# The last segment's attention in the turned form of the other three, a whole-product output projection, and 64-column products in the spectral stage

## The chip, the cores and the metric

The kernel runs on one core of a Trainium2 chip. The metric is the device time of one execution in microseconds (us), the median of several; a profile of a single execution is beside it. The engines are PE (matrix products), PEld (its weight loads), DVE, ACT and POOL (elementwise work), and SP, which here only issues transfers.

## The reference

The input x is 2048 tokens of 640 features in bf16. Two branches are computed from it and mixed by a gate per token.

```python
def _A_ref(x, wq, wk, wv, wo, beta):          # H=32 heads of 20, N=4 segments of L=512
    q, k, v = heads(x @ wq), heads(x @ wk), heads(x @ wv)
    phi = lambda t: jnp.where(t > 0, t + 1.0, jnp.exp(t))
    g = _sigmoid(beta).reshape(1, H, 1, 1)
    for s in range(N):
        logits = jnp.einsum('bhqd,bhkd->bhqk', qs, ks) * scale + mask      # causal in the segment
        a_dot = softmax(logits) @ vs
        a_mem = (phi(qs) @ M) / (phi(qs) @ z + 1e-06)
        outs.append(g * a_mem + (1.0 - g) * a_dot)
        M, z = M + phi(ks).T @ vs, z + phi(ks).sum()
    return o @ wo

def _B_ref(x, w_r, w_i):
    return irfft2(rfft2(x) * (w_r + 1j * w_i))

g = _sigmoid((x * gate_w).sum(-1, keepdims=True))
return g * _A_ref(...) + (1 - g) * _B_ref(...)
```

## The kernel before

**Stages.** The kernel works through four segments s = 0 to 3 of 512 tokens. For each, `project` multiplies x with wq, wk and wv; q and k go through a scratch in memory (`qk_scr`) and come back as rows of one head each (`qkp`), and the values stand in `va`. `mem_read` computes the memory's part (`mem`), `attend` the softmax attention. Branch B (`fft`) is a series of matrix products with tables (`Ac`, `Bt`, `tt`, `Wt`, `Cp`, `big`), whose result stands in `G`; one of them, here called the D product, multiplies `Ac` with `big`. Its pieces are laid between the segments' work all along.

**Attention.** Eight groups of four heads make up a segment, two groups a pair. A pair has five units (`qk_unit`): the products q·k of a unit fill the four PSUM banks of the pool "qk", and ACT takes the exponential of all four (L1508, into `ex`), so each unit waits until the one before it has been read. POOL or DVE set the masked corners to zero (L1540 and L1549, L1539 and L1545). Then the values:

- For segments 0 to 2 `pv_flipped` (L1407): 20 products a group in which the values stand and the probabilities stream, on 32-column tiles of the array, one a head. Their result has a head's 20 values and its sum in rows. It is evicted to `ub`, written to memory (`u_scr`) by pairs, and read back as the features in order (`oU`) and as the sums of all heads (`dnc`, in `denominators`, L1431). The sums are inverted (L1440), joined with the gates (`rc`, L1442) and spread over the features by four products (`spread`, L1446) whose eviction is `r`; `oU` is multiplied by `r` (L1791). The memory's part goes through `o_scr`, is read back transposed (`mT`) and added (L1799).
- For segment 3 `pv_group` (L1556): 40 products a group in which the probabilities stand and 21 columns of values and ones stream. Result and sums lie beside each other, so the division follows at once (`rs`, `on`, L1587 to L1592), `mem` is added (L1597), and `last_transposes` (L1756) turns `on` by 20 products into `oTl`.

**The end.** `finish_tile` (L1773) makes the output of 128 tokens in two halves. One bank collects eight products on 32-column tiles of `G` with the gate's columns (`fbg`, `fbn`) and then the output projection, five chunks of `oU` or `oTl` with `wo`, each chunk in four pieces on 32-column tiles (L546 where a function splits it, L548 for segment 3). The sum is evicted as `ot` and written out.

**Order.** The program is recorded as operations with their dependences; the class `Sched` puts them on the engines in the order of a table of numbers (`ORDER`, L741; `ENDED`, L615, says which end frees a bank), and turns dependences into semaphores. Each engine runs its own row strictly in that order, and so does the queue of transfers that it issues: nearly all are SP's. PE has modes by the shape of its tiles: whole (0), 32-column tiles (2), the q·k shapes (1) and 64-column tiles (4).

Of the kernel before, what the change touches and what calls it, by code (L numbers as in the profile page):

```python
# [9 lines left out]
BF = dt.bfloat16  # L10
# [34 lines left out]
class Op:  # L45
    __slots__ = ("id", "alts", "preds", "succs", "prio", "banks", "nbytes", "npred", "eng", "t0", "t1",
                 "stamp", "rank", "need_inc", "dyn", "first", "outside", "name", "dma", "key", "xfer", "lock", "mode", "emode", "hold", "width", "high", "follow")


class Sched:  # L50
# [9 lines left out]
    def op(self, alts, r=(), w=(), prio=0.0, nbytes=0, name="", after=(), dma=False, xfer=0.0, lock=False, mode=0, hold=False, width=16):  # L60
# [4 lines left out]
        o.high, o.follow = False, None  # L65
# [47 lines left out]
    def schedule(self, pools, order, ended, nsem=56):  # L113
# [17 lines left out]
        for p, o in zip(queue["pool"], queue["pool"][1:]):  # L131
            if p.high != o.high:
                o.follow = p
        pe, held = queue["pe"], {}
        for i, o in enumerate(pe):
            o.emode = o.mode
            if o.mode < 0:
                modes = [held[id(b)] for b in o.banks if id(b) in held]
                if not modes and i and pe[i - 1].emode not in (1, 4):
                    modes = [pe[i - 1].emode]  # L140
                for q in pe[i + 1:] if not modes else ():
                    m = q.mode if q.mode >= 0 else held.get(id(q.banks[0]), -1)
                    if m >= 0:
                        modes = [0 if m == 1 else m]
                        break
                o.emode = (modes + [0])[0]
            if o.emode not in (1, 4):
                for b in o.banks:
                    held[id(b)] = o.emode
# [6 lines left out]
        sems = [[0.0, i, None] for i in range(nsem)]  # L156
        issued = []
        self.order = []
# [49 lines left out]
        while len(self.order) < len(order):  # L208
# [19 lines left out]
            if e == "pe" and o.emode != mode:  # L228
                occ += self.COST[mode, o.emode]
                mode = o.emode  # L230
# [3 lines left out]
            if o.dma:  # L234
                if o.hold:
                    free[e] = max(free[e], max(ring) + 170.0)
                for q in range(o.width):
                    ring[q] = max(ring[q], free[e] + 1300.0) + o.xfer
# [6 lines left out]
                sems.sort(key=lambda q: (q[0], q[1]))  # L245
                sm = sems[0]
# [13 lines left out]
        self.nsem = nsem  # L260
# [235 lines left out]
class Kern:  # L496
# [35 lines left out]
    def mms(self, items, r, w, prio, name="", extra=0.0, mode=0):  # L532
# [861 lines left out]
    def attend(self, s):  # L1394
# [9 lines left out]
        if s < 3:  # L1404
            self.denominators(s)
# [469 lines left out]
```

## Time and profile before

| | |
|---|---|
| median of three runs | 243.16 us (242.58 to 244.0) |
| the profiled execution's own time | 242.17 us |
| its span | 240.4 us, so 1.8 us lie around it |
| PE, DVE, ACT, POOL busy | 95%, 85%, 84%, 39% of the span |
| granted clock of PE | 1.00 throughout |
| transfers | 43.46 MB in 58072 packets |

Rows of groups read: line, engine, operation, output<-inputs, how many | busy us, mean ns of one | idle time of the engine before them, and what ended it. PE's means overlap, since products are pipelined: what one costs is read from the start of a row to the start of the next. Rows of the timeline read: start, busy us, engine and group, and in brackets the idle time before. Rows of transfers end with the median us from issue to landing.

### The profile page before, as it was taken

What the parts mean: (1) busy time and instruction counts of PE and PEld (TensorE: products, weight loads), DVE (VectorE), ACT (ScalarE), POOL (GpSimd) and SP (SyncE); (2) the same over time, 40 slices, a digit from 0 to 9 for tenths busy, and PEclk for the clock granted to TensorE, in tenths of its full rate; (3) what the DMA queues carried; (4) which work ended last, traced back from release to release, by engine and by line L of the source; (5) the groups of instructions that cost most, each with busy time, mean ns of one, the idle gap of its engine ahead of it and who ended that gap; (6) DMA issues with size and microseconds to landing.
All of it is one profiled execution on the core that took longest, in us unless ns stands there. A gap on an engine that the chain in (4) does not pass through costs nothing.

```text
span 240.4 us, 10161 instructions
## 1 busy us (share of the span) xinstructions
PE 228.9 (95%) x4361; PEld 146.3 (61%) x4361; DVE 203.8 (85%) x493; ACT 202.7 (84%) x253; POOL 92.9 (39%) x172
## 2 busy tenths in 40 slices
PE   7999799999999999999989999999999999999993
PEld 4666367666556674654656555565555667667883
DVE  0978888999999899999999999899999679747742
ACT  2398979999999999999999999899899977678630
POOL 5203415503655407250516733504546232272810
PEclk9999999999999999999999999999999999999999
DMA  7998988678979989849986748378759862782213
GB/s 195 373 182 264 198 270 176 148 239 211 213 146 241 221 215 226 200 136 154 216 246 162 229 129 223 92 197 201 197 154 223 209 151 79 105 90 92 77 43 108
DMA packets 58072, 43.46 MB, mean 181 GB/s; under 512 B 27628, under 2 KB 55724, under 8 KB 58028
## 3 DMA queue, kind: packets, MB, share of 16 engines
q1 hardware_dynamic: 57500, 42.46, 73.9%
q8 instruction: 34, 0.56, 1.0%
q10 hardware_dynamic: 528, 0.36, 0.5%
q14 instruction: 10, 0.08, 0.1%
HBM read 22.73 MB, written 12.20 MB: 145 GB/s over the span
## 4 chain that ended last, share of the span: by engine, by line
PE 60%; DVE 15%; ACT 12%; DMA 6%; SPq 3%; issue 3%; DVEq 0%
PE psum L548 53%; ACT ex L1508 9%; PE psum L546 7%; DMA hm<-tab_hmask 3%; DMA qk_scr<-qu 2%; SPq L582 2%; DMA u_scr<-ub 2%; DVE mem L1389 1%; DVE G L559 1%; DVE oU L1791 1%; DVE ub L559 1%; DVE ex L1545 1%; DVE Pt L1696 1%; ACT qu L557 1%; DVE dn L1381 1%
## 5 line engine op out<-in xcount | busy, mean ns | idle before, releaser
L1508 ACT ACTIVATE ex<-psum 128x2048 bf16<-128x2048 f32 (+4 forms) x92 | 138.6, 1507 | 12.2 <-PE psum L548 10.7
L1549 POOL TENSOR_SCALAR_AFFINE_SELECT ex<-ex 64x256 bf16<-64x256 bf16 x66 | 26.8, 427 | 64.3 <-ACT ex L1508 63.5
L1540 POOL TENSOR_SCALAR_AFFINE_SELECT ex<-ex 128x512 bf16<-128x512 bf16 x44 | 29.4, 678 | 31.7 <-DVE ex L1545 20.3
L548 PE MATMUL psum<-qkp 20*64 20x64 bf16 (+5 forms) x1024 | 31.4, 266 | 1.6 <-ACT ex L1508 0.9
L548 PE MATMUL psum<-wv,xT 128*64 128x320 bf16 (+3 forms) x240 | 26.6, 302 | 2.4 <-DMA wv<-in_A_wv_dram 1.5
L548 PE MATMUL psum<-xT,wk 128*128 128x256 bf16 (+1 forms) x280 | 28.3, 273 | 0.0
L548 PE MATMUL psum<-xT,wq 128*128 128x512 bf16 (+1 forms) x135 | 27.9, 380 | 0.0
L1696 DVE TENSOR_TENSOR Pt<-psum,Wt 128x644 bf16<-128x644 f32 x32 | 25.8, 820 | 1.4 <-PE psum L548 1.1
L548 PEld LDWEIGHTS psum<-xT,wk 128*128 128x128 bf16 (+1 forms) x280 | 20.9, 98 | 4.4 <-issue 0.4
L548 PEld LDWEIGHTS psum<-qkp 20*64 20x64 bf16 (+1 forms) x1024 | 12.1, 100 | 18.1 <-ACT ex L1508 10.9
L546 PE MATMUL psum<-wo,oU 128*32 128x320 bf16 x480 | 21.0, 299 | 0.0
L548 PEld LDWEIGHTS psum<-wv,xT 128*64 128x64 bf16 (+1 forms) x240 | 14.8, 105 | 9.4 <-DMA wv<-in_A_wv_dram 1.7
L559 DVE CAST ot<-psum 128x320 bf16<-128x320 f32 x20 | 9.4, 489 | 10.3 <-PE psum L546 4.5
L548 PE MATMUL psum<-ex,va 128*32 128x512 bf16 (+4 forms) x480 | 17.3, 274 | 0.1
L548 PE MATMUL psum<-big,Cp 128*128 128x321 bf16 (+1 forms) x96 | 16.7, 302 | 0.7 <-DVE rs L1587 0.3
L548 PE MATMUL psum<-tt,Pt 128*128 128x128 bf16 (+1 forms) x192 | 16.4, 221 | 0.0
L1298 ACT ACTIVATE et<-qu 128x512 bf16<-128x512 bf16 x25 | 15.6, 629 | 0.4 <-DVE phk L1311 0.4
L546 PEld LDWEIGHTS psum<-wo,oU 128*32 128x32 bf16 x480 | 12.8, 97 | 3.8 <-issue 0.6
L548 PE MATMUL psum<-big,Ac 128*32 128x160 bf16 (+2 forms) x384 | 14.4, 259 | 0.7 <-DVE mem L1385 0.5
L1545 DVE TENSOR_TENSOR ex<-ex,hm 128x512 bf16<-128x512 bf16 (+1 forms) x31 | 13.8, 453 | 1.3 <-ACT ex L1508 1.0
L548 PEld LDWEIGHTS psum<-tt,Pt 128*128 128x128 bf16 (+1 forms) x192 | 12.1, 102 | 4.4 <-issue 0.9
L548 PEld LDWEIGHTS psum<-xT,wq 128*128 128x128 bf16 (+1 forms) x135 | 9.2, 97 | 8.5 <-issue 1.8
(114 smaller groups left out, 420.6 us busy)
## 6 DMA issues: line engine op xcount, KB each, us to landing
qkp<-qk_scr SPq DMA_DIRECT2D x28, 160.0 KB
qk_scr<-qu SPq DMA_DIRECT2D x12, 256.0 KB, 3.6
tt<-tab_tt SPq DMA_DIRECT2D x8, 384.0 KB, 4.4
u_scr<-ub SPq DMA_DIRECT2D x12, 256.0 KB, 3.6
Wt<-Wt SPq DMA_DIRECT2D x8, 321.0 KB, 4.0
xsb<-in_A_x_dram SPq DMA_DIRECT2D x8, 320.0 KB, 5.4
oU<-u_scr SPq DMA_DIRECT2D x15, 128.0 KB, 3.2
out_dram<-ot SPq DMA_DIRECT2D x12, 160.0 KB
```

The source lines that it names most:

```text
L546: h = e.matmul(dst, wt, r_, start=st, stop=sp_, **{**kw, "tile_position": (0, q), "skip_group_check": True})
L548: h = e.matmul(o_, l_, r_, start=st, stop=sp_, **kw)
L557: alts["act"] = (lambda e: e.activation(dst(), src(), ACT.Copy), 65 + 0.833 * n, 110.0)
L559: alts["dve"] = (lambda e: e.tensor_copy(dst(), src()), 67 + 1.04 * n, 68.0)
L582: return e.dma_start(d_, s_)
L1298: self.one("act", lambda e: e.activation(et.ap(0, [1, L]), qsl(), ACT.Exp), L, [qb], [b("et", pi_)], late, fix=94, name="phi_exp")
L1381: self.one("dve", lambda e: e.reciprocal(dn.ap(32, [1, 32]), dn.ap(0, [1, 32])), 32, [b("dn", i % 2, q) for q in range(2)], [rb], prio, fi ...
L1508: self.one("act", lambda e, d=d, q=q: e.activation(self.ex.ap(*d), self.ps(bank, *q), ACT.Exp, scale=SC), n, [bank], [self.exb(s, 2 * pr + ...
L1540: pick = lambda e: e.affine_select(ex(), ex(), [[0, 4], [1, P]], ALU.is_ge, 0.0, base=0, channel_multiplier=-1)
L1545: least = lambda e: e.tensor_tensor(dst(), src(), self.hm.ap(880 + 64 * t, [0, 4], [0, 2], [1, 64], np_=nd), ALU.min)
L1549: h = e.affine_select(self.ex.ap(e0 + d, [1280, 4], [1, 64], p0=hp, np_=np_), self.ex.ap(e0 + q, [1280, 4], [1, 64], p0=hp, np_=np_), [[0, ...
L1696: self.one("dve", lambda e, x=x, Pt=Pt, Wt=Wt, wo_=wo_, bank=bank: e.tensor_tensor(Pt.ap(x * 644, [322, 2], [161, 2], [1, 161]), self.ps(b ...
```

## The change

1. Segment 3 uses `pv_flipped`, `denominators`, `spread`, the transposed reading of its memory part and the multiplications and additions of the other segments; `pv_group` and `last_transposes` with their tiles are gone. Its exponentials and masks take the layout of the others, so that units whose exponential was split in two (1280 and 768, 512 and 512 columns a partition row) are one again. Two of its five reads of `oU` are issued by ACT.
2. The output projection is one whole product a chunk (128 rows, 128 columns, 320 streamed) for all segments: 160 products for 640 pieces.
3. The D product: 64-column tiles in mode 4, two side by side, 192 products for 384.
4. `qk_scr` holds q and k of a feature as one row, so that a read has runs of 2 KB for 1 KB, and one write of 128 rows takes the place of two of 64.
5. `gate_w` is loaded as five contiguous rows, transposed by PE and evicted, in place of 640 elements of two bytes.
6. The writes `st_out` (12) and `st_o` (12) are issued by POOL, and 14 others too (weights, tables, gates): 38 transfers in POOL's order, where there were none.
7. The tables of the order are new, and the planner's rules, which only make these tables' meaning.

```diff
@@ mms
-                if op.mode < 0 and op.emode == 2:
-                    m, pitch = l_.ap[1][1], l_.ap[1][0]
-                    for q in range(0, m, 32):
...
-                        h = e.matmul(dst, wt, r_, start=st, stop=sp_, **{**kw, "tile_position": (0, q), "skip_group_check": True})
-                else:
-                    h = e.matmul(o_, l_, r_, start=st, stop=sp_, **kw)
+                h = e.matmul(o_, l_, r_, start=st, stop=sp_, **kw)
@@ dma
-        queues = ("sp", "act") if name in self.EARLY else (queue,)
+        queues = ("sp", "act") if name in self.EARLY else ("sp", "pool") if name in self.SPARE else ("pool",) if name in ("st_out", "st_o") else (queue,)
...
+    SPARE = ("ld_W", "dup_W", "ld_tt", "ld_gw", "ld_beta", "ld_hm", "ld_big", "ld_wv", "ld_x", "ld_wo", "ld_g", "ld_gc", "ld_den", "st_g")
@@ alloc
-        self.qkd = nc.dram_tensor("qk_scr", (NSEG, 2, 2, 320, L), BF)
+        self.qkd = nc.dram_tensor("qk_scr", (NSEG, 640, 2, L), BF)
-        self.ud = nc.dram_tensor("u_scr", (3, 1024, L), BF)
+        self.ud = nc.dram_tensor("u_scr", (4, 1024, L), BF)
@@ record
         self.gate_table(3)
-        self.last_transposes()
+        self.spread(3)
@@ loads
-        self.dma(lambda: self.wv.ap(D, [D + 1, 5], [1, 1]), lambda: dap(self.gw_d, 0, [1, P], [P, 5], [1, 1]),
-                 P * 5 * 64, [], [self.b("gw")], 0.31, name="ld_gw")
+        self.dma(lambda: self.dnc.ap(0, [1, P], np_=5), lambda: dap(self.gw_d, 0, [P, 5], [1, P]), 5 * 256, [], [self.b("dnc")], 0.31, name="ld_gw")
...
+                 [self.b("dnc"), self.b("id"), bank], [], 0.5, name="gwT", mode=1)
@@ attend
             for g in (2 * pr, 2 * pr + 1):
-                if s < 3:
-                    self.pv_flipped(s, g)
-                else:
-                    self.pv_group(s, g)
-        if s < 3:
-            self.denominators(s)
+                self.pv_flipped(s, g)
+        self.denominators(s)
@@ fft
-                        for q in range(4):
+                        for q in range(2):
...
-                            return (self.ps(bank, c0, [1, n], p0=32 * q, np_=32), self.Ac.ap(c * 2048 + GROUPS[g] * P + x * 64 + q % 2 * 32, [1, 32]),
+                            return (self.ps(bank, c0, [1, n], p0=64 * q, np_=64), self.Ac.ap(c * 2048 + GROUPS[g] * P + x * 64, [1, 64]),
@@ finish_tile
-                if s < 3:
-                    def th(c=c, hf=hf, bank=bank):
-                        return (self.ps(bank, 0, [1, 320]), oT.ap(c * L + a * P, [1, P]), self.wo[c].ap(hf * 320, [1, 320]), False, c == 4,
-                                {"skip_group_check": True})
...
-                self.mms(items, [b("oTl", c), b("wo2"), bank] if s == 3 else [ob[c], b("wo", c), bank], [], prio, name="oproj", mode=2 if s == 3 else -1)
+                self.mms([(th, 320)], [ob[c], b("wo", c), bank], [], prio, name="oproj", mode=0)
```

How the order moves at three places. On PE, in the last rows of before, the products of segment 3's values and their transposes stand ahead of its gate and output products (`va,ex` are values, `fcat,on` transposes, `G,fbg` and `G,fbn` gate products, `wo,oU` segments 0 to 2's output and `wo,oTl` segment 3's):

```order
L546 MATMUL psum<-wo_112,oU_113 32x320 x4
L548 MATMUL psum<-va_107,ex 128x21 x80
L548 MATMUL psum<-fcat,on 128x128 x4
L548 MATMUL psum<-G,fbg_70 32x320 x4
L548 MATMUL psum<-G,fbn_81 32x320 x4
L548 MATMUL psum<-wo_88,oTl 32x320 x8
```

Now, after the last turned group, PE has output products of the other segments (`oU_77`, `oU_112` and `oU_113`; `oU_85` is segment 3's), the spreading of segment 3's sums (`rc_125,hm`) and the gate products, and only then segment 3's output:

```order
L541 MATMUL psum<-wo_108,oU_113 128x320
L541 MATMUL psum<-rc_125,hm 128x128 x4
L541 MATMUL psum<-wo_109,oU_113 128x320
L541 MATMUL psum<-wo_110,oU_113 128x320
L541 MATMUL psum<-wo_111,oU_113 128x320
L541 MATMUL psum<-G,fbg_72 32x320 x4
L541 MATMUL psum<-G,fbn_83 32x320 x4
L541 MATMUL psum<-G,fbg_70 32x320 x4
L541 MATMUL psum<-G,fbn_81 32x320 x4
L541 MATMUL psum<-G,fbg_70 32x320 x28
```

What moved: output products of segments 0 to 2 from ahead of the last values to behind them, and a wait for `rc` into the middle of PE's row. On DVE the last rows of the changed kernel, from the last masks (`ex`) to the first addition of the memory part (`mT`), are:

```order
L1489 TENSOR_TENSOR ex<-ex,hm 128x4x128
L553 CAST G<-psum 128x321
L1408 RECIPROCAL dnr<-dnc 128x128
L1410 SCALAR_TENSOR_TENSOR rc_125<-dnr,ebx,gcc 128x128
L1229 TENSOR_SCALAR fbn_81<-fbg_70 128x512
L553 CAST r_95<-psum 128x512
L1679 TENSOR_TENSOR oU_85<-oU_85,r_95 128x512 x5
L1687 TENSOR_TENSOR oU_85<-oU_85,mT_80 128x5x128
```

These seven steps behind the masks follow each other by their data, where before `rs`, `on` and `oTl` stood. On POOL, towards the end, the masks of the exponentials (`ex`) and the gate's columns (`fbg`) now stand among transfers:

```order
L1490 AFFINE_SELECT ex<-ex 128x4x128
L576 DMA o_scr<-mem 8x16x640
L1225 TENSOR_TENSOR fbg_72<-fcat,gbc 128x512
L576 DMA out_dram<-ot_73 4x32x640
L1687 TENSOR_TENSOR oU_113<-oU_113,mT_78 128x5x128
L576 DMA o_scr<-mem 8x16x640
L576 DMA out_dram<-ot_74 4x32x640
```

Before, the same stretch of POOL's row had masks, additions of `mem` to `on` (L1597) and no transfer.

More of the change, by code (lines that the diff above doesn't have):

```diff
@@ L64, in op @@
         o = Op()
[L65 removed]
+        o.high, o.follow, o.count = False, None, 0
         o.id = len(self.ops)
@@ L130, in schedule @@
                 b.left = len(b.ops)
-        for p, o in zip(queue["pool"], queue["pool"][1:]):
+        own = [o for o in queue["pool"] if not o.dma]
+        for p, o in zip(own, own[1:]):
             if p.high != o.high:
                 o.follow = p
[L134 to L149, printed above, removed]
         pos = {e: 0 for e in self.eng}
@@ L156, in schedule @@
         sems = [[0.0, i, None] for i in range(nsem)]
+        stream, pieces = 0.0, []
         issued = []
+        self.nsem = nsem
         self.order = []
```

287 lines of the change are left out of this document (100 added, 187 removed), and 496 rows, old and new, of tables (ENDED, ORDER, PIECES).

## The prediction

> **What bounds the kernel now.** I read the shares of the page first, then the busy time of each engine by stretches, then the exponentials alone, then the timeline of the last 20 us.
>
> ```profile
> PE 228.9 (95%) x4361; PEld 146.3 (61%) x4361; DVE 203.8 (85%) x493; ACT 202.7 (84%) x253; POOL 92.9 (39%) x172
> ...
> 40.00:180.00 140.00, 136.26 (x2426) 82.66 (x2422) 133.16 (x323) 134.08 (x160) 58.27 (x114) 1.00 0.79 190
> 180.00:200.00 20.00, 19.23 (x436) 11.98 (x425) 16.43 (x41) 17.47 (x23) 8.62 (x14) 1.00 0.77 186
> 200.00:225.30 25.30, 25.07 (x752) 18.28 (x756) 18.16 (x44) 19.43 (x22) 10.12 (x19) 1.00 0.51 89
> 225.30:240.40 15.10, 11.53 (x340) 10.11 (x332) 7.03 (x17) 3.77 (x8) 3.12 (x4) 1.00 0.26 77
> ```
>
> The columns are length, then busy time of PE, PEld, DVE, ACT and POOL, clock, DMA share and GB/s. From 40 to 180 us PE, DVE and ACT are all above 95%: little can be won there by moving work. From 180 us ACT (17.47 of 20, 19.43 of 25.3) and DVE have room and PE has none. After 225.3 us almost only PE works. The change alters the last segment, so the question is two spans: when the last exponential ends, and how long the program needs after it.
>
> ```profile
> 223.16 2.08 ACT L1508 ACTIVATE ex<-psum 128x1280 bf16<-128x1280 f32 x2 [0.33 <-PE psum L548]
> 226.01 2.17 PE L548 MATMUL psum<-va,ex 128*128 128x21 bf16 x80
> 228.04 0.38 PE L548 MATMUL psum<-fcat,on 128*128 128x128 bf16 x4
> 236.87 0.49 DVE L559 CAST ot<-psum 128x320 bf16<-128x320 f32 x1 [0.46 <-PE psum L548]
> ```
>
> The last exponential ends at 223.16 + 2.08 = 225.24; everything up to the span's end at 240.4 is the **tail**, 15.2 us: values, transposes, 40 x 4 pieces of the output projection, and from the last eviction (236.87) another 3.5 us to write the output.
>
> **The change, part by part.** First PE. The 320 products of segment 3 with 21 columns are 80 in 228.04 - 226.01 = 2.03 us, so 8.1 us in all.
>
> ```profile
> L548 PE MATMUL psum<-big,Ac 128*32 128x160 bf16 (+2 forms) x384 | 14.4, 259 | 0.7 <-DVE mem L1385 0.5
> ...
> 177.27 1.70 PE L548 MATMUL psum<-big,Cp 128*128 128x321 bf16 x11 [0.27 <-DVE r L559]
> 178.90 0.32 PE L548 MATMUL psum<-qkp 20*64 20x64 bf16 x24
> 179.67 0.73 PE L548 MATMUL psum<-ex,va 128*32 128x512 bf16 x20
> ...
> 208.22 1.40 PE L546 MATMUL psum<-wo,oU 128*32 128x320 bf16 x36
> 209.54 0.43 PE L548 MATMUL psum<-qkp 20*64 20x512 bf16 x12
> ...
> 222.40 0.38 PE L548 MATMUL psum<-fcat,on 128*128 128x128 bf16 x4
> 222.71 0.40 PE L548 MATMUL psum<-qkp 20*128 20x320 bf16 x8
> 229.97 0.62 PE L548 MATMUL psum<-fcat,on 128*128 128x128 bf16 x8
> 230.52 0.73 PE L548 MATMUL psum<-G,fbg 128*32 128x320 bf16 x16
> ```
>
> The turned form takes 20 products a group; 0.73 less about 0.2 of modelled end is 0.53, eight groups 4.3: **3.8 us less**. The 20 transposes go too: 8 cost 0.55 and 4 cost 0.31, so one is 0.06 and the switch of tile shape beside them 0.07: 20 are 1.2 us, less 0.2 for one more spreading: **1.0 less**. The output projection: 36 pieces take 1.32, so four are 0.147 with the switch in it; a whole product of nearly that shape is (178.90 - 177.27)/11 = 0.148 with a switch in it: **0**. D in tiles of 64 columns: half as many products, two side by side instead of four. Before shows no such product; the bounds are half of the first row's 14.4 us gone, 7.2, and nothing or a little more (the columns that pass are the same). The nearest pair of rows, output pieces against whole products, says **0**. Whole products stand between 32-column gate products in every half tile, so the shape changes twice each time: by the order 40 switches more, at 0.07 to 0.10 **+2.8 to +4**. PE's sum: -3.8 - 1.0 + 0 + 3.5 = **-1.3 us**: small.
>
> The Trainium skill, page "TensorEngine Tiling (Array Packing)", section "Tiling Modes", states that a change of tiling mode drains TensorE, which speaks against this alternation; the 0.07 between the rows above agrees with it and is the whole price seen here, while the page gives none.
>
> Second, how early the exponentials end. The order puts less work ahead of the last q·k products: behind them stand 85 whole output products, 128 gate products, 9 of the last big stage and two turned groups; before, 55 output products' worth, 88 gate products, 80 of 21 columns and 12 transposes. By the prices above that is 85 x 0.14 + 32 x 0.14 + 1.3 + 1.1 + 18 x 0.08 = 20.2 us against 55 x 0.14 + 22 x 0.14 + 2.0 + 0.7 + 0.4 = 13.9 (four gate pieces 0.14): PE comes to the last unit **6 to 7 us sooner**. ACT must follow.
>
> ```profile
> 180.00:200.00 20.00, 13.73 (x12) 1.00 0.77 186
> 200.00:225.30 25.30, 17.72 (x16) 1.00 0.51 89
> ...
> L1508 ACT ACTIVATE ex<-psum 128x2048 bf16<-128x2048 f32 x56 | 105.2, 1878 | 6.9 <-PE psum L548 6.2
> L1508 ACT ACTIVATE ex<-psum 128x1280 bf16<-128x1280 f32 x8 | 9.9, 1241 | 2.8 <-PE psum L548 2.8
> L1508 ACT ACTIVATE ex<-psum 128x1024 bf16<-128x1024 f32 x12 | 12.3, 1022 | 0.6 <-PE psum L548 0.3
> L1508 ACT ACTIVATE ex<-psum 128x768 bf16<-128x768 f32 x8 | 6.5, 810 | 0.3
> L1508 ACT ACTIVATE ex<-psum 128x512 bf16<-128x512 f32 x8 | 4.8, 596 | 1.5 <-PE psum L548 1.4
> ...
> 185.54 0.43 PE L548 MATMUL psum<-qkp 20*64 20x512 bf16 x12
> 186.06 1.88 ACT L1508 ACTIVATE ex<-psum 128x2048 bf16<-128x2048 f32 x1
> ```
>
> The two windows are of L1508 alone: 31.45 us of exponentials from 180 to 225.3. They belong to 18 units; a unit takes the same four banks as the one ahead, so its products start when that exponential is read out and ACT waits at least 186.06 - 185.54 = 0.52, with the hop 0.55 (the evictions of about 0.44 fit into that). Nine of the units are no longer split: 1241 + 810 against 1878 and 2 x 596 against 1022 is 0.17 each, 1.6 in all. The floor is 31.45 - 1.6 + 18 x 0.53 = 39.4 against 45.2 now: **5.8 us sooner**, so the last exponential ends at about 219.4. PE's 6 to 7 is just enough for it.
>
> Third, the tail. The turned form has its sums in rows, and they go through memory: values evicted (ub), written (u_scr), the denominators read back (dnc), inverted, spread by PE, evicted (r), multiplied into five tiles, the memory read added. For segments 0 to 2 this lay under other segments' attention; for segment 3 it is behind the last exponential.
>
> ```profile
> L1539 DVE TENSOR_TENSOR ex<-ex,hm 128x512 bf16<-128x512 bf16 x20 | 10.7, 544 | 2.0 <-ACT ex L1508 1.9
> L559 DVE CAST ub<-psum 128x512 bf16<-128x512 f32 x16 | 10.8, 677 | 0.2 <-DMA u_scr<-ub 0.2
> u_scr<-ub SPq DMA_DIRECT2D x12, 256.0 KB, 3.6
> DMA to landing us min/median/max: 2.0/2.0/2.0
> L1440 DVE RECIPROCAL dnr<-dnc 128x128 f32<-128x128 bf16 x3 | 2.8, 944 | 0.0
> L1442 DVE SCALAR_TENSOR_TENSOR rc<-dnr,ebx,gcc 128x128 bf16<-128x128 f32 x3 | 1.0, 345 | 0.0
> L559 DVE CAST r<-psum 128x512 bf16<-128x512 f32 x3 | 2.0, 677 | 0.0
> L1791 DVE TENSOR_TENSOR oU<-oU,r x13: 406/416/1216, 175.0 to 201.7; 128x512 bf16<-128x512 bf16 x13
> L1799 DVE TENSOR_TENSOR oU<-oU,mT 128x640 bf16<-128x640 bf16 x8 | 4.2, 542 | 0.3 <-DMA mT<-o_scr 0.3
> ```
>
> The fourth row is the denominators' tile; the last row but one gives minimum, median and maximum. The sum: two masks 1.1, products 0.7, ub 0.65, write 3.6, read 2.0, reciprocal 0.95, rc 0.35, the fbn that DVE has in between 0.3, spreading 0.3, r 0.68, five products at 0.42 2.1, one addition 0.54: 13.3 us until PE may start segment 3's output. PE's 85 - 40 products of other segments and the gate products fill about 10 of them. Then 40 products at 0.14 and two gate pieces, 6.0, and 3.5 + 0.4 from the last product to the end: 13.3 + 6.0 + 3.9 = 23.2, and by the write at 3.0 in a quiet memory 22.6. I take **22.7 against 15.2: 7.5 later**. Behind the waiting spread on PE stand 7 output and 64 gate products (3.3 us by the prices above); they run while DVE evicts r, multiplies and adds (0.68 + 2.1 + 0.54), and then nothing is left, so a later spread delays the end by its whole delay.
>
> The other edits I cost at nothing: POOL gives some masks to DVE and segment 3's old normalisation leaves it (493 instructions become 480), within the 10.7 us that DVE stands idle in the two windows from 180 to 225.3; the four more transposing reads of the memory and the fewer, longer q/k transfers are SP's, which issues 212 transfers for 241. If DVE's room were gone, 14 more masks at 0.54 would be 7.6 us of its time.
>
> Sum against the profiled run: 240.4 - 5.8 + 7.5 = 242.1 span, and 242.17 - 240.4 = 1.8 around it 243.9. The start can give something back: PE waits there for wv, behind the load of gate_w in two-byte pieces.
>
> ```profile
> 29.37 3.71 PE L548 MATMUL psum<-wv,xT 128*128 128x320 bf16 x45 [1.49 <-DMA wv<-in_A_wv_dram]
> PEld psum L548 <- issue: 15.5, 67, 0.7
> ```
>
> That wait is 1.5 us; gate_w as five runs and q/k rows of 2 KB may remove between none and all of it. From 40 us on all engines are full, so I credit 0.3: 243.6 for a run such as the profiled one. The median shown (243.16) is 1.0 above the profiled run's 242.17, so the **forecast is 244.6**, 0.6% slower.
>
> **Rivals.** (a) Forecast: the memory round trip of the last segment outweighs the shorter stream; 243 to 246.5. (b) Faster: PE alone decides. Its sum is 1.3 lower; the wv wait goes (1.5); and the sequencer's waits shown above, 15.5 us of 67, are mostly for instructions not yet there, so with a fifth fewer products (3514 for 4361) up to 3 us of them go. For it speaks that PE is at 95%; against it that the last segment's chain above is serial. With half of those 3, PE's 4.3 us would give 238.9; the chain holds that up: a stream that ends at 217 and a tail of 21, its write and read at their fastest, give 217 + 21 + 1.8 + 1.0 = 240.8. So 239.5 to 242. (c) Slower by more: the POOL queue. POOL now issues 38 transfers between its masks, and before has none, so no row prices one. SP's rows of 0.4 to 0.6 us are the nearest from below: 38 x 0.5 = 19 us on an engine with 147 us free, nothing. From above:
>
> ```profile
> L1791 POOL TENSOR_TENSOR oU<-oU,r x2: 1146/1146/1147, 180.8 to 181.9; 128x512 bf16<-128x512 bf16 x2
> ```
>
> While POOL worked on the same kind of product (1.15 us), DVE's took up to 1.2 us instead of 0.42 (its row stands above): the two shut each other out. If an issue lasts 1.2 us and holds DVE so, 38 x 0.8 = 30 us of DVE time, a third of it on a path with 95% full engines: 248 to 252. It decides once an issue passes about 1 us. I take the SP row, since nothing here shows the other. The Trainium skill, "SBUF — State Buffer", section "Who interferes with whom", states that a transfer issued from GpSimd waits while VectorE holds the shared port; by its figures (620 ns alone, about 3100 beside a copy) the 38 would estimate at up to 94 us more on POOL, and no run here shows it. (d) The change does nothing: the 7.5 is paid by 5.8 and the 1.5 at the start, 243.4, or 242 to 244.4.
>
> **Chances.** (a) 0.42, (b) 0.28, (c) 0.08, (d) 0.22. A measurement tells 0.5% (1.2 us) from no change: faster than 241.9 takes (b), about 0.29 with a little of (d); between 241.9 and 244.4 (d) and a part of (a), 0.29; slower 0.42. The range leaves out (c)'s upper end and (b)'s lower: 240.0 to 248.0. The forecast's own range is 243 to 246.5.
>
> **What would show it.** Right: the last exponential near 219.4 and PE standing idle or nearly so between the last other products and the first product of wo with segment 3's oU, which starts 13 us after that exponential. Wrong: exponentials before 217.5 (the floor fell earlier, at the start), a round trip under 4 us, POOL rows of over 1 us for an issue, masks late behind them, or 32-column and whole products alternating at more than 0.1 us a switch.

## The result and the profile after

The changed kernel takes 261.6 us (median of 4 runs, 256.53 to 266.14) against 243.58 for the kernel before beside it: 1.0602 times as long, 95% interval 1.045 to 1.0755. (The ratio leaves out runs with a disturbed clock, so it lies below the quotient of the medians.) The forecast was 244.6, 0.6% slower, with a range of 240.0 to 248.0: the direction came out as forecast, the size is ten times as large. The profiled run took 256.53 us with a span of 254.8, 14.4 more than before's 240.4.

The page's first line and the busy time by stretches, cut as before's were (stream to the last exponential, then the tail):

```profile
PE 229.1 (90%) x3504; PEld 134.7 (53%) x3514; DVE 204.0 (80%) x480; ACT 204.6 (80%) x253; POOL 101.6 (40%) x185
...
180.00:200.00 20.00, 17.11 (x279) 8.13 (x277) 18.48 (x38) 16.26 (x16) 8.18 (x9) 1.00 0.77 187
200.00:228.10 28.10, 24.71 (x410) 12.45 (x410) 18.94 (x46) 22.83 (x25) 8.68 (x11) 1.00 0.62 110
228.10:254.80 26.70, 18.96 (x249) 10.95 (x241) 8.89 (x20) 6.82 (x17) 6.59 (x8) 0.99 0.51 125
```

PE is as busy in sum as before, with a fifth fewer instructions, and from 180 us on it has holes: 17.11 of 20 and 24.71 of 28.1, where before had 19.23 of 20 and 25.07 of 25.3. The tail is 26.7 us long, not 15.2. The timeline of the tail (a row with x2 or more runs from the start of its first to the end of its last, so the 10.49 us of the row `mT` hold two issues and the time between them):

```profile
226.26 1.88 ACT L1466 ACTIVATE ex<-psum 128x2048 bf16<-128x2048 f32 x1 [1.67 <-PE psum L541]
...
228.56 2.25 SPq L576 DMA_DIRECT2D u_scr<-ub  x2
235.19 10.49 SPq L574 DMA_TRANSPOSE mT<-o_scr  x2
236.78 0.95 DVE L1408 RECIPROCAL dnr<-dnc 128x128 f32<-128x128 bf16 x1 [7.15 <-DMA dnc<-u_scr]
...
238.18 0.40 PE L541 MATMUL psum<-rc,hm 128*128 128x128 bf16 x4 [1.11 <-DVE rc L1410]
...
239.34 1.77 DVE L1679 TENSOR_TENSOR oU<-oU,r 128x512 bf16<-128x512 bf16 x5
...
243.95 0.89 DVE L1687 TENSOR_TENSOR oU<-oU,mT 128x640 bf16<-128x640 bf16 x2 [2.84 <-DMA mT<-o_scr]
244.50 4.38 PE L541 MATMUL psum<-wo,oU 128*128 128x320 bf16 x31 [2.56 <-DVE oU L1687]
```

The last exponential ends at 226.26 + 1.88 = 228.14, against 225.24 before and 219.4 in the forecast. The round trip itself is as worked out: the five products by r end at 241.11, 13.0 us after that exponential; the prediction's terms up to there gave 12.8. Then DVE waits 2.84 us for `mT`, the memory part read by columns. The tile view of `mT`, after and then before:

```profile
L574 SPq DMA_TRANSPOSE mT<-o_scr x12: 1201/1254/2451, 169.0 to 244.5; - x12
...
  DMA mT<-o_scr: 6.6, 3
...
DMA to landing us min/median/max: 2.8/4.7/10.7
```

```profile
L580 SPq DMA_TRANSPOSE mT<-o_scr x8: 1199/1268/2360, 165.2 to 212.1; - x8
...
  DMA mT<-o_scr: 0.3, 1
```

The first row gives minimum, median and maximum of one issue in ns, and the first and last start. A transposing read is issued in the same 1.25 us in both, by the median; but after has twelve, the last ones lie among segment 3's own transfers, and its slowest lands 10.7 us after its issue (the one landing on record in before took 4.1). DVE waits 6.6 us for them in place of 0.3.

The other place is the stream. Counting the 80 units from 0, the exponentials lead those of before by 2.6 us at unit 5 (the wait for `wv` is gone) and by 2.9 at unit 14, and are 0.4 late at unit 18. There, at 62.43 us, PE waits 1.24 us for `Pt`, and the windows behind it show a lower clock (last number but two):

```profile
62.00:64.00 2.00, 1.48 (x19) 0.69 (x23) 2.00 (x5) 0.83 (x2) 1.94 (x4) 0.72 1.00 186
64.00:66.00 2.00, 1.78 (x34) 0.81 (x28) 1.24 (x3) 1.21 (x3) 1.93 (x5) 0.50 1.04 194
```

From there on the lag grows to 2.9 us at unit 63, is 5.0 at the next unit, 0.6 thirteen units later, and 3.1 at the last. The timeline around unit 64, 183 to 188 us, after:

```profile
183.44 1.15 POOL L1679 TENSOR_TENSOR oU<-oU,r 128x512 bf16<-128x512 bf16 x1 [1.48 <-DVE r L553]
183.47 1.39 DVE L1679 TENSOR_TENSOR oU<-oU,r 128x512 bf16<-128x512 bf16 x1
184.79 1.84 DVE L1495 TENSOR_TENSOR ex<-ex,hm 64x512 bf16<-64x512 bf16 x1
185.18 1.16 POOL L1679 TENSOR_TENSOR oU<-oU,r 128x512 bf16<-128x512 bf16 x1
187.10 1.00 PE L541 MATMUL psum<-big,Cp 128*128 128x321 bf16 x6 [2.23 <-DVE G L553]
```

While POOL makes two of these products, two operations of DVE last 1.39 and 1.84 us where others of their kind take 0.42, and PE waits 2.23 us for an eviction behind them. From there to unit 77 the exponentials gain 4.4 us on before (5.0 late to 0.6), as the forecast's ACT floor wanted. Then, DVE:

```profile
217.30 0.89 DVE L553 CAST ot<-psum 128x320 bf16<-128x320 f32 x2 [0.85 <-DMA out_dram<-ot]
...
220.59 0.89 DVE L1687 TENSOR_TENSOR oU<-oU,mT 128x640 bf16<-128x640 bf16 x2 [1.99 <-DMA mT<-o_scr]
...
223.87 0.49 DVE L1687 TENSOR_TENSOR oU<-oU,mT 128x640 bf16<-128x640 bf16 x1 [1.79 <-DMA mT<-o_scr]
```

In DVE's row the masks and evictions that free the last exponentials' banks stand behind these waits.

Two theories were put to the test first: that the twelve transposing reads, among other transfers, hold these up and are held up; and that the transfers on POOL's queue are late. Two more came from the traces: that waits of PE lower its clock, and that POOL's products beside DVE cost a unit.

### The profile page after: what moved, and what is told of

Read it like the earlier page. It is cut to its first block, busy times and chain, and to the rows that moved or that the text cites. A ratio compares the mean times of both kernels' runs of the same rounds, so it can differ in the third digit from the quotient of the medians.

```text
span 254.8 us, 8434 instructions
## 1 busy us (share of the span) xinstructions
PE 229.1 (90%) x3504; PEld 134.7 (53%) x3514; DVE 204.0 (80%) x480; ACT 204.6 (80%) x253; POOL 101.6 (40%) x185
## 3 DMA queue, kind: packets, MB, share of 16 engines
q0 software_dynamic: 3536, 6.57, 10.7%
## 4 chain that ended last, share of the span: by engine, by line
PE 41%; DVE 17%; DMA 16%; ACT 15%; issue 3%; SPq 3%; POOL 3%; DVEq 0%; POOLq 0%
PE psum L541 41%; ACT ex L1466 12%; DMA mT<-o_scr 4%; DVE mem L1361 3%; SPq L576 3%; DMA Wt<-in_B_w_i_dram 2%; DMA wk<-in_A_wk_dram 2%; DMA gcc<-g_scr 2%; DMA out_dram<-ot 2%; DVE Pt L1601 2%; DMA dnc<-u_scr 2%; DVE ex L1495 2%; DVE dn L1358 1%; DVE oU L1679 1%; DVE ex L1489 1%
## 5 line engine op out<-in xcount | busy, mean ns | idle before, releaser
L1466 ACT ACTIVATE ex<-psum 128x2048 bf16<-128x2048 f32 (+1 forms) x80 | 136.7, 1709 | 19.9 <-PE psum L541 18.4
L1490 POOL TENSOR_SCALAR_AFFINE_SELECT ex<-ex 128x512 bf16<-128x512 bf16 x35 | 23.6, 681 | 27.1 <-DVE ex L1495 18.6
L1499 POOL TENSOR_SCALAR_AFFINE_SELECT ex<-ex 64x256 bf16<-64x256 bf16 x56 | 22.7, 428 | 25.8 <-ACT ex L1466 25.4
L541 PE MATMUL psum<-wo,oU 128*128 128x320 bf16 x160 | 26.0, 300 | 2.6 <-DVE oU L1687 2.6
L541 PE MATMUL psum<-ex,va 128*32 128x512 bf16 (+4 forms) x640 | 23.7, 279 | 3.4 <-DVE ex L1489 1.5
L541 PE MATMUL psum<-xT,wq 128*128 128x512 bf16 (+1 forms) x125 | 24.6, 381 | 1.6 <-DMA wq<-in_A_wq_dram 0.5
L541 PEld LDWEIGHTS psum<-wo,oU 128*128 128x128 bf16 x160 | 14.1, 98 | 12.2 <-issue 4.2
L551 ACT ACTIVATE ot<-psum 128x320 bf16<-128x320 f32 x20 | 8.5, 437 | 13.8 <-PE psum L541 13.7
L541 PEld LDWEIGHTS psum<-ex,va 128*32 128x32 bf16 x640 | 11.9, 97 | 14.4 <-DVE ex L1489 3.2
L541 PE MATMUL psum<-big,Ac 128*64 128x322 bf16 (+2 forms) x192 | 14.8, 267 | 1.7 <-DVE Pt L1601 1.3
L576 POOL DMA_DIRECT2D out_dram<-ot x12 | 8.4, 699 | 16.9 <-ACT ot L551 10.2
```

The source lines that it names most:

```text
L541: h = e.matmul(o_, l_, r_, start=st, stop=sp_, **kw)
L551: alts["act"] = (lambda e: e.activation(dst(), src(), ACT.Copy), 65 + 0.833 * n, 110.0)
L576: return e.dma_start(d_, s_)
L1466: self.one("act", lambda e: e.activation(self.ex.ap(off, *d), self.ps(bank, 0, *q), ACT.Exp, scale=SC), n, [bank], [self.exb(s, 2 * pr + g ...
L1490: pick = lambda e: e.affine_select(ex(), ex(), [[0, 4], [1, P]], ALU.is_ge, 0.0, base=0, channel_multiplier=-1)
L1499: h = e.affine_select(self.ex.ap(e0 + d, [1280, 4], [1, 64], p0=hp, np_=np_), self.ex.ap(e0 + q, [1280, 4], [1, 64], p0=hp, np_=np_), [[0, ...
```

## The experiments

Times are medians; each ratio is to the kernel before, run on the same chip.

**The queue.** `e1_all_sp`: the changed kernel with POOL's 38 transfers issued by SP, each put in by its planned time. `e2_before_stores_pool`: the reverse, the kernel before with its 20 stores of the memory part and the output on POOL. The edit of e1:

```
+            for o in [o for o in queue["pool"] if o.dma and o.name in ('st_out', 'st_o', 'ld_W', ...)]:
+                queue["pool"].remove(o)
+                o.eng = "sp"
+                q = queue["sp"]
+                q.insert(len([p for p in q if self.when[p.id] <= self.when[o.id]]), o)
```

> The changed kernel with all 38 transfers of POOL's row issued by SP again, each at the place of SP's row that its planned time gives; all else, the order of the other engines too, as changed. Theory A (the POOL queue is what costs the 14 us: transfers issued there land late and everything that waits for them or lies beside them is late): 243 to 247 us, the transposing reads of mT land within 4 us, the last exponential ends at 218 to 222. Theory B (the turned last segment with its transposing reads and its trip through memory costs it, whoever issues): 252 us or more, mT still at 7 us or more.

> The kernel before with its 20 stores st_o and st_out issued by POOL, at the places of POOL's row that their planned times give. Theory A: slower by 3 to 9 us (246 to 252), half to two thirds of what 38 cost. Theory B: no change, 242.5 to 244.5.

e1: 256.04, 1.0555 [1.0484, 1.0627]; e2: 252.99, 1.0297 [1.0162, 1.0432]. The two don't agree: in before the queue costs 3%, in after next to nothing comes back (the intervals of e1 and of the changed kernel overlap). e1's stream is 2.9 us faster (last exponential 225.2), but its tail is 28.6 us. The time is theory B's, though `mT` isn't: its three landings on record take 3.6 to 5.3 us. The windows of e1's tail (the clock is the last number but two), and PE's row:

```profile
234.00:236.00 2.00, 0.14 (x2) 0.00 (x0) 0.00 (x0) 0.34 (x1) 0.00 (x0) 1.00 0.80 243
236.00:238.00 2.00, 0.00 (x0) 0.00 (x0) 1.27 (x3) 0.00 (x0) 0.00 (x0) 0.68 1.12 178
238.00:242.00 4.00, 3.92 (x47) 2.24 (x51) 3.43 (x10) 0.44 (x1) 0.69 (x1) 0.50 0.26 79
242.00:244.00 2.00, 2.00 (x34) 0.98 (x23) 1.37 (x1) 0.00 (x0) 1.02 (x1) 0.61 0.70 137
```

```profile
238.09 0.61 PE L551 MATMUL psum<-rc,hm 128*128 128x128 bf16 x4 [3.94 <-DVE rc L1420]
...
240.47 2.08 PE L551 MATMUL psum<-G,fbg 128*32 128x320 bf16 x28
```

PE runs out of other work and waits 3.94 us for the denominators; the granted clock then falls to 0.5, and 28 gate products take 2.08 us where the changed kernel's take 1.13. e2 shows the same in mid-kernel (windows, then the rows at the wait):

```profile
152.00:156.00 4.00, 1.35 (x34) 0.85 (x30) 2.18 (x5) 1.91 (x2) 1.85 (x4) 1.00 0.17 54
156.00:160.00 4.00, 4.00 (x34) 1.77 (x31) 2.86 (x5) 2.14 (x4) 0.00 (x0) 0.57 0.34 98
```

```profile
153.82 0.83 DVE L1711 TENSOR_TENSOR Pt<-psum,Wt 128x644 bf16<-128x644 f32 x1 [2.95 <-DMA Wt<-Wt]
154.70 0.73 PE L563 MATMUL psum<-ex,va 128*32 128x512 bf16 x20 [2.65 <-DVE Pt L1711]
```

The load of `Wt` that DVE waits for was issued by SP between two of POOL's stores and landed after 7.9 us; in before the slowest on record takes 5.4. So a late transfer can cost its delay and a slower clock behind it. Not every such wait does: in the changed kernel PE waits 2.23 us at 187.10 and 2.56 at 244.50, and the clock stays at 1.00. Rival (c)'s threshold is not what decides: an issue on POOL takes 0.6 to 0.8 us in the traces, and the 38 together take 25 us, far from the prediction's estimate of up to 94 more.

**Parts of the change alone, in the kernel before.** Whole output products for segments 0 to 2 (e3); D in 64-column tiles (e4); q/k by rows (e5); the last two together (e11).

```
-                if op.mode < 0 and op.emode == 2:        # e3
+                if False:
-                    for q in range(4):                   # e4, and tiles of 64 for 32
+                    for q in range(2):
-        self.qkd = nc.dram_tensor("qk_scr", (NSEG, 2, 2, 320, L), BF)      # e5
+        self.qkd = nc.dram_tensor("qk_scr", (NSEG, 640, 2, L), BF)
```

> The kernel before with the output projection of segments 0 to 2 in whole products (120 for 480), everything else and the whole order kept. By the prediction's prices (whole against pieces 0, two more switches of tile shape a half tile at 0.07 to 0.10): 1.7 to 2.4 us slower where PE is the bound, so 244.5 to 246. If a switch is hidden behind the weight load: no change, 243 to 244.

> The kernel before with the D products on 64-column tiles (192 for 384), order kept. The prediction's value is 0: 242.5 to 244. If half the products save their issue time, up to 3 us faster.

> The kernel before with q and k of a feature as one row of the scratch (reads in runs of 2 KB), nothing else; its writes stay two of 64 rows. The changed kernel's exponentials run 3.5 us ahead of before's at the 12th unit. If the q/k rows give that start: units 5 to 12 are 1 to 3 us ahead here and the time is 0.5 to 2 us shorter (241 to 242.5). If the start came from the 64-column D products alone (whose run alone is 1.4 us ahead there): no change.

> The kernel before with the 64-column D products and the q/k rows of the change, and nothing else of it. The D run was 1.1% faster than before, the rows' run the same as before. Expected: 0.8 to 1.5% faster than before, so faster than both kernels.

e3: 244.07, 1.0095 [1.0052, 1.0138]: about +2.3 us, so the alternation of shapes is paid as priced. e4: 241.93, 0.9892 [0.9797, 0.9988]; e5: 242.0, 0.9993 [0.9953, 1.0034]; e11: 241.48, 0.9967 [0.993, 1.0004]. e4's 1.1% rests on two executions; e11, which has the same D products, shows 0.3% in ten, against the 0.8 to 1.5% expected. The trace says that e4's lead isn't D's: its exponentials are 1.4 us ahead of before's at unit 5, though the first D product starts at 56.5 us, and 1.3 ahead at unit 63, when the last is done; before's wait of 1.49 us for `wv` isn't there. And the D products, 14.4 us in before, take no less in e4:

```profile
L548 PE MATMUL psum<-big,Ac 128*64 128x161 bf16 (+2 forms) x192 | 14.6, 263 | 0.4 <-DVE mem L1385 0.3
```

So neither D's wider tiles nor the rows show a gain of their own. Of these parts only e3's costs anything, about 1%.

**The tail's two waits.** `e6_mt_first` sets one of segment 3's transposing reads ahead of the last two writes of `u_scr`; `e7_sp_busy` is e1 with 56 idle products where PE would stand waiting (they write into columns beside the sums, and some results come out changed); `e8_sp_busy_mt` joins both.

```
+        sp.remove(oT[-2])                                 # e6
+        sp.insert(sp.index(oT[-3]) + 1, oT[-2])
+        for k, n in ((i, 40), (j[0], 16)):                # e7
+                for _ in range(n):
+                    self.nc.tensor.matmul(self.ps(bank, 320, [1, 192]), self.fcat.ap(P, [1, P]), self.wo[0].ap(0, [1, 192]), ...)
+            pe[k].pre = pre
```

> The changed kernel with one of segment 3's transposing reads (the first of the last two of mT) ahead of the last two writes of u_scr in SP's row instead of behind the reads of oU. In the changed kernel it lands at 243.9, 8.7 us after its issue, and DVE and then PE wait 2.8 and 2.6 us for it. Theory C (the tail is long because its transfers collide: dnc 4.1, mT 8.7 us): the wait goes, the profiled span is 2 to 2.5 us shorter for the same end of the exponentials. Theory D (the serial steps of the chain alone set the tail): the wait moves to the next step, under 0.5 us.

> The first experiment's kernel (all transfers on SP) with 40 idle products of 192 columns on PE ahead of the wait for segment 3's spreading and 16 ahead of its first output product; they write columns that nobody reads. In the first experiment PE stood 3.9 us there, its clock was granted at 0.50 from 238 to 242 and 64 gate products took 5.2 us. Theory E (a wait of PE of some 2.5 us or more costs the clock for the next 4 to 6 us, at half speed): the clock stays 1.0 in the tail and the tail is 2 to 3 us shorter, 253 to 254. Against it: the idle products delay the chain, 256 or more.

> The kernel of the run before with segment 3's transposing read moved forward as well. If C and E both hold: 251 to 253. If only E: as the run before.

e6: 259.7, 1.0696 [1.0619, 1.0773]: the tail's wait for `mT` is gone, but DVE then waits 1.79 us for a read of `oU` from `u_scr`, until 243.85, and no time is won. e7: 255.7, 1.0569 [1.0473, 1.0664]; e8: 255.52, 1.044 [1.0368, 1.0512]. In e7 the tail's clock stays at 1.00, but 40 idle products hold the spread up by 3.1 us, since the denominators had come sooner than in e1; the tail is 26.4 us against 28.6, the span 252.0 against 253.8. e8's tail is 26.4 too. So moving one read only changes which transfer is late.

**The transposing reads themselves.** The same bytes read plain, which leaves the transposition out, so that the memory's part is added in the wrong order: segment 3's four in the changed kernel (e9) and in e1 (e10); all twelve in e1 (e12); and, as a control, all eight in the kernel before (e15). e13 is e12 and e14 is e1 with eight tiles `ot` for four.

```
-                     [b("od", s, i) for i in range(4)], [mb], prio - 8.5, tr=True, name="oT", after=self.after_mid(("mT", k3)))
+                     [b("od", s, i) for i in range(4)], [mb], prio - 8.5, name="oT", after=self.after_mid(("mT", k3)))      # e12, e15; tr=s < 3 in e9, e10
-        k4 = self.finc % 4      # e13, e14
+        k4 = self.finc % 8
```

> The changed kernel with segment 3's four transposing reads of its memory part (mT) made plain reads of the same 160 KB each: the transposition is left out, so the last 512 tokens' memory part is added in the wrong order. Theory F (the four added transposing reads, which the prediction set at nothing, hold up the transfers of the last 45 us: mT lands 7 to 9 us after its issue, DVE waits 6.6 us for it, and the last three exponentials and the tail are late for that): DVE's waits for mT fall below 2 us, units 77 to 79 keep 2.4 us apart (7.0 us late in the changed kernel), the tail from the last exponential is 23 to 24 us for 26.7: 4 to 7 us shorter, a median of 251 to 256. Theory G (they only fill idle queues): within 1.5 us of the changed kernel.

> The first experiment's kernel (all transfers on SP) with the same four reads made plain. If both the POOL queue and the transposing reads cost, and the costs add: 247 to 251. If only the POOL queue's place was lost to SP's own waits: 254 or more.

> The first experiment's kernel (all transfers on SP) with all twelve transposing reads of the memory part made plain reads of the same bytes (the transposition left out, so the memory part of segments 1 to 3 is added in the wrong order). Theory H (a transposing read among other transfers holds up all of them: with segment 3's own writes now between them, out_dram, u_scr and mT land 6 to 8 us after issue from 206 to 224): out_dram, u_scr and mT land within 4 us, DVE does not wait for out_dram, the last exponential ends at 219 to 222, 245 to 249. Theory I (the amount of traffic is what counts): as with four plain reads, 252 to 255.

> The same with eight output tiles ot for four, so that an eviction of ot need not wait for the output write of four tiles before. If H holds: within 1 us of the run before, since nothing waits there any more. If I holds: 2 to 4 us shorter than the run before.

> The first experiment's kernel with eight output tiles ot, transposing reads as changed. DVE waited 2.2 us there (3.2 with four plain reads) for output writes to land, in its row ahead of the masks and the ub of the last units. If that wait makes the last three exponentials late: they end 2 to 3 us sooner and the time is 253 to 254. If DVE then waits for mT instead: 255 to 256.

> Control: the kernel before with its eight transposing reads of the memory part made plain (transposition left out, so the memory part of segments 1 and 2 is added in the wrong order). Before, nothing but gate and output transfers stands among them and DVE waits 0.3 us for them. By H: within 0.5% of before. If transposing reads cost by themselves: 2 us or more shorter.

e9: 258.38, 1.0534 [1.0449, 1.062]; e10: 253.94, 1.0445 [1.0376, 1.0514]. Segment 3's four alone bring about 1% or less, not clear of the intervals; e10's timeline shows why:

```profile
214.97 5.07 SPq L584 DMA_TRANSPOSE mT<-o_scr  x1
...
218.46 0.89 DVE L563 CAST ot<-psum 128x320 bf16<-128x320 f32 x2 [3.24 <-DMA out_dram<-ot]
```

One of the other segments' reads occupies SP for 5.07 us instead of 1.25, and DVE waits 3.24 us for a store of the output. e12: 248.58, 1.0257 [1.0187, 1.0326], 3.0% or 7.2 us less than e1 by the ratios; e15: 242.44, 1.0012 [0.9971, 1.0053]. In the traces of e1, e10 and e12 every engine and SP's row have the same order, so nothing but the kind of the reads differs. The tile view of `mT` in e12 and its last exponential:

```profile
L586 SPq DMA_DIRECT2D mT<-o_scr x12: 326/428/881, 166.5 to 234.8; - x12
...
DMA to landing us min/median/max: 3.2/3.5/4.2
```

```profile
220.36 1.88 ACT L1476 ACTIVATE ex<-psum 128x2048 bf16<-128x2048 f32 x1 [0.21 <-PE psum L551]
```

The same reads, plain, land in at most 4.2 us, the last exponential ends at 222.24 (e1: 225.21) and the tail is 245.2 - 222.24 = 23.0 (e1: 28.6). In before the same edit is worth nothing. What the reads held up in e1 is not `mT`, for which DVE waits only 0.8 us there, but what stands behind them in SP's row. The tail of e1, then of e12:

```profile
223.57 3.27 SPq L584 DMA_TRANSPOSE mT<-o_scr  x1
226.90 0.48 SPq L586 DMA_DIRECT2D g_scr<-gT  x1
230.36 0.60 SPq L586 DMA_DIRECT2D gcc<-g_scr  x1
231.67 0.57 SPq L586 DMA_DIRECT2D dnc<-u_scr  x1
236.69 0.95 DVE L1418 RECIPROCAL dnr<-dnc 128x128 f32<-128x128 bf16 x1 [9.97 <-DMA dnc<-u_scr]
```

```profile
219.67 0.43 SPq L586 DMA_DIRECT2D mT<-o_scr  x1
226.69 0.57 SPq L586 DMA_DIRECT2D dnc<-u_scr  x1
```

In e1 the store of the gate and its reading back (`g_scr`, `gcc`) follow a read whose issue lasts 3.27 us, and the denominators' read `dnc`, behind them in the row, is issued 6.5 us after the last exponential and takes 5.0 us to DVE's reciprocal; in e12 these are 4.5 and 3.2 (the reciprocal starts at 229.89). e13: 248.86, 1.0248 [1.0155, 1.0342], and e14: 254.49, 1.0537 [1.0479, 1.0594]: eight `ot` tiles change neither time. In e14 DVE no longer waits for the output's stores (2.2 us in e1), but 1.9 us for `mT`; these waits were not what decided.

**POOL's two products.** POOL's products of `oU` and `r` given to DVE, in e12 (e16) and in the changed kernel itself (e17).

```
+            for o in [o for o in queue["pool"] if o.name == "normal"]:
+                queue["pool"].remove(o)
+                o.eng = "dve"
+                q = queue["dve"]
+                q.insert(len([p for p in q if self.when[p.id] <= self.when[o.id]]), o)
```

> The twelve plain reads, all transfers on SP, and in addition POOL's two products oU = oU x r (2.4 us on POOL from 180.1) are made by DVE, the first one behind the next eviction of G; nothing else moves. It adds the memory part in the wrong order, as before. Theory of the shared port: while POOL makes these two products, two DVE operations beside them last 1.40 and 1.37 us instead of 0.42 each, PE waits 1.75 us for G at 183.28, the exponential of that unit comes at 184.74 after a wait of 1.51, and behind the thin stretch from 180 to 184 the clock is 0.73 and 0.50 until 188. Without it DVE has 2 x 0.42 more and 1.9 less, PE's wait falls to under 0.8, the exponential starts at 183.0 to 183.8, the clock stays 1.0 from 184 to 188, and the last exponential ends at 219.5 to 221 instead of 222.2. Time 246 to 247.5 instead of 248.6. Rival, the order itself: the unit is late by the evictions of G that stand together in the order; the wait stays at 1.2 or more and the time within 0.7 us of 248.6.

> The changed kernel, with POOL's two products oU = oU x r made by DVE, nothing else. In the changed kernel's profile the two DVE operations beside them last 1.39 and 1.84 us instead of 0.42 and PE waits 2.23 us for G at 187.10. Theory of the shared port: that wait falls below 1 us and the exponentials from there to unit 77 come 0.5 to 2 us sooner; but the transposing reads hold up the transfers behind it all the same, so the last exponential ends at most 1.5 us sooner and the time is 259 to 262 against 261.6. Rival, the stall at 187 is a full term of the sum: 257 to 259. Rival, the order: no change of the wait.

e16: 245.53, 1.0126 [1.0057, 1.0195]; e17: 258.53, 1.0578 [1.0494, 1.0662]. DVE and PE in e16, then its last exponential:

```profile
181.64 0.42 DVE L1694 TENSOR_TENSOR oU<-oU,r 128x512 bf16<-128x512 bf16 x1
181.98 0.41 DVE L1510 TENSOR_TENSOR ex<-ex,hm 64x512 bf16<-64x512 bf16 x1
...
182.03 2.14 PE L556 MATMUL psum<-big,Cp 128*128 128x321 bf16 x12
...
219.90 1.88 ACT L1481 ACTIVATE ex<-psum 128x2048 bf16<-128x2048 f32 x1 [0.21 <-PE psum L556]
```

DVE's two operations take 0.42 and 0.41, PE makes its twelve products without a stop, and the clock stays at 1.00 from 184 to 188 us, where e12 has 0.73 and 0.50:

```profile
184.00:186.00 2.00, 2.00 (x27) 0.63 (x25) 2.00 (x6) 1.26 (x1) 0.76 (x1) 0.73 0.85 206
186.00:188.00 2.00, 2.00 (x24) 0.64 (x22) 1.54 (x5) 0.62 (x1) 0.77 (x1) 0.50 0.45 111
```

Against e12 the exponentials are 1.5 us late ahead of this place, 1.3 early behind it and 0.5 early at the end (221.8): 2.8 won, of which 2.0 stay. In e17 they come 2.2 us sooner too, and give it all back behind:

```profile
217.36 0.89 DVE L563 CAST ot<-psum 128x320 bf16<-128x320 f32 x2 [2.57 <-DMA out_dram<-ot]
```

The last exponential ends at 228.2 as without the edit. Two causes lie one behind the other on one path; taking the first away alone brings nothing.

## Why the prediction was wrong, step by step

The failing step is the sentence that cost the other edits at nothing, in its words "the four more transposing reads of the memory" on SP. It counted issues (212 for 241) and looked at SP's room; the row it had, 0.3 us of waiting for `mT`, came from eight reads in another place. The runs put about 7.2 us in its place (e1 to e12, 1.0555 to 1.0257). And the cost isn't that of the four added reads alone: by the ratios they bring 2.7 us (e1 to e10, not clear of the intervals), the eight that the kernel had before bring 4.6 more (e10 to e12). e15 shows that those eight cost nothing in before, so what is left is their place among the transfers of the changed kernel. The step took the place of an issue in SP's row as free, because SP had room on the whole; in e1 an issue of up to 3.27 us stands ahead of the transfers that the last exponentials and the round trip wait for.

The profiled spans account for the miss: 254.8 against 242.1 in the forecast's sum is 12.7. Unit 55, at some 163 us, lies ahead of the first of these reads; there after is already 1.6 us later than e16. Of the rest, -0.3 goes with POOL's queue (after to e1), 7.2 with the transposing reads (e1 to e12; 1.6 of them ahead of the last exponential's end, 5.6 behind it), 1.8 with POOL's two products (e12 to e16), and 2.4 are left. These are single executions, with the causes taken away in this order. The 2.4 are stream: e16's last exponential ends at 221.8 against 219.4, and 1.25 of them stand at unit 62 already (180.60 against 179.34 in before), where the forecast's floor began.

- PE's sum of -1.3: the switches of shape cost what they were priced at (e3: +2.3 for segments 0 to 2, against 1.7 to 2.4 by those prices). D at 0 was right: 14.6 us of products against 14.4.
- The stream: ACT's floor was the right bound where nothing held it up (4.4 us gained in thirteen units of after; the last sixteen units of e16 start within 36 us). What was late was its beginning and, in after, its end. "The 10.7 us that DVE stands idle" was no cover for a wait for a transfer in the middle of its row.
- The tail of 22.7: right as a mechanism and in size where the transfers aren't held up: e16's is 244.5 - 221.8 = 22.7, though a shorter way to the products by r (11.8 for 12.8) and a longer one behind them offset each other. In after that first part took 13.0 and in e1 16.0. What failed in after is the addition's input: `mT` was given no time of its own, and the wait of 2.84 us for it is most of the 4.0 by which after's tail passes the forecast.
- The direction was no luck: with the transposing reads and POOL's products out of the way (e16) the stream is 3.5 us shorter than in before, the tail 7.5 longer, and the time 1.3% longer, as the forecast has it in kind.
- Rival (b), PE alone: wrong; PE's holes from 180 us on show that it didn't decide. Its term for the sequencer fails too: the weight loads' waits on "issue", 15.5 us in before, are 24.6 in e3 with 3989 products and 21.6 in after with 3504, so fewer products did not shorten them. Rival (c), the POOL queue: its end of the range was nearest, by another mechanism. Its threshold of 1 us an issue wasn't reached. The row it quoted, POOL's and DVE's products in each other's way, did count, without any transfer: about 1.3% in e12 (e16; the intervals just touch). The Trainium skill, "SBUF — State Buffer", section "Who interferes with whom", states that a VectorE operation with two inputs in SBUF contends with a GpSimd one that reads SBUF; 1.39 and 1.84 us for 0.42 agree.
- The start credit of 0.3: after leads by 2.6 us at unit 5 and has lost it by unit 18, so nothing of it reached the last segment; how much the rows and the load of gate_w have to do with it, the runs do not show apart.

Left open: the 2.4 us of stream; how much of after's order alone is in them; whether the turned segment alone, in before's order, would be as slow; and gate_w's load. These weren't tried. Nor was POOL's queue with plain reads: since e2 shows 3% for it in before, the nothing that e1 shows can be a cost hidden behind the reads. Why a plain read passes where a transposing one is held, the trace doesn't say; it shows only issues of up to 5.07 us and landings of up to 10.7. No form of the turned last segment was faster than before; e4 (0.9892) and e11 (0.9967, whose interval reaches 1.0004), which leave segment 3 alone, were the quickest kernels.

## What to carry to other kernels

A transfer that costs nothing in one place can cost in another, where stores and a round trip run: price a moved or added transfer by what else is in flight there and by what stands behind it in its queue's row, not by the count of issues. This holds for the transfers that the kernel already had as much as for the added ones. Work of the last stage that goes through memory needs other work behind it for the round trip and for everything that the trip meets. When an edit removes one wait and nothing changes, look for a second on the same path before dropping the theory: e10 and e17 each took away a true cause and showed little of it.

## What the runs showed of the hardware

- **Transposing reads among other transfers.** In before an issue takes 1.27 us (median; at most 2.36), and the one landing on record 4.1 us; plain reads in its place 0.46 and 3.7 (e15). Among segment 3's transfers an issue took up to 3.27 us in e1 and 5.07 in e10, and a read up to 10.7 us to land in the changed kernel; plain, at most 0.88 and 4.2 (e12). The Trainium skill, "Advanced Engine Details and Errata", section "X-Bar Transpose (TRN2)", states that they are as fast as regular transfers: e15 agrees, e12 against e1 does not (7.2 us).
- **Stores issued by POOL.** Those of the output took up to 8.8 us to land in the changed kernel and 6.6 in e2; issued by SP or ACT, at most 3.3 of those on record in e1 and 2.6 in before.
- **The clock after thin stretches.** A wait of PE of 2.65 us (e2) was followed by a clock of 0.57 over four us, one of 3.94 (e1) by 0.50, one of 1.75 (e12, 183.28) by 0.73 and 0.50, one of 1.24 (the changed kernel, 62.43) by 0.50. But 2.23 and 2.56 us in the changed kernel left it at 1.00, so the length of one wait does not decide it. The Trainium skill, "TensorE: Matmul & The Clock Gate", section "HAM oscillation — how this bites in real kernels", warns of gaps over about 3.4 us; here less was enough at times.
- **DVE and POOL.** Two products of 1.15 us on POOL took 2.4 us from DVE (1.39 + 1.84 for 2 x 0.42) and through PE a unit's 2.2 us.
